# A three-stage fp32 network on one core: the gates of two token blocks from seven products of halves in place of eight

## The chip, the cores and the metric

One core of a Trainium2 chip runs the whole program in one launch. The metric is the device time of one execution in microseconds (us): the median of three runs is 1384.78 us.

## The reference

Retention attention (8 heads, 576 positions, 8 sequences) gives `x`; a mixer adds a low-rank mix of positions and a 512-2048-512 ReLU layer; a last stage makes the output. Its lines, on 4608 tokens (8 x 576) of 512 features:

```python
x_prev = np.concatenate([np.zeros((B, 1, D), dtype=np.float32), x[:, :-1, :]], axis=1)
xk = mu_k * x + (1.0 - mu_k) * x_prev
xr = mu_r * x + (1.0 - mu_r) * x_prev
k = np.maximum(xk @ w_k, 0.0)
v = k * k @ w_v
r = 1.0 / (1.0 + np.exp(-(xr @ w_r)))
return (r * v).astype(np.float32)
```

The change touches `r`: the product of `xr` with the 512 x 512 weight `w_r`, called the gates.

## The kernel before, in words

Features lie on the 128 partitions, tokens along the free axis, in 9 blocks of 512 tokens. Every fp32 product is made of three fp32r matmuls (128 x 512 out): the operands are split into a high half (a cast on ACT) and a low half (a subtraction on DVE or POOL), and weight high x token high, weight low x token high, weight high x token low are added in PSUM. Every instruction stands in its engine's queue in the order in which the Python code issues it (`manual_schedule`, L1002), so a waiting instruction holds back all that come after it on its engine.

Three stages follow one another. Up to about 565 us the attention, the low-rank mix and the first layer run; weights of later stages come in as 64-bit floats and are converted beside them, by jobs in the list `waiting`, of which `slot` (L135) runs one stage of each job that is under way. A job is load, `down` (ACT), `fill` (DVE), splits, and a store of the halves to DRAM ("parked"). `w_r` is parked by `Weight.park` (L172), `w_k` by `key_weight` (L208) with the four sums of its quarter blocks that products of halves need. `second_weight` (L348) brings in the weights of the second layer. Up to about 870 us the second layer runs over four pairs of blocks, seven products of half blocks for eight (`products`, L488); then the ninth block is done plainly (`project`, L583) to 914 us.

From 914 us on the last stage goes over the four pairs of blocks (L1316), then over the ninth block alone:
- `gate_tile` (L1186) makes the gates of one block and one quarter of the features: 12 matmuls into one PSUM bank, then a sigmoid on ACT. A pair has 8 of these, so 96 matmuls. Its weights `wru` stay in SBUF from 880 us to the end.
- `key_group` (L1207) makes one of four groups of 256 key features of both blocks, by seven products of halves of 6 matmuls each, and its results are squared and split (`square`, L1199). Its weights `wk` are fetched for each group.
- `value_part` (L1266) multiplies one group's squares with `w_v`, 24 matmuls into four banks `v`; after the fourth part of a block DVE multiplies `v` with the gates (L1284) and the result goes out.

The order for a pair is: 8 gate tiles, key groups 0 and 1, value part 0 of the even block, key group 2, value part 1, key group 3, value parts 2 and 3, then four value parts of the odd block. The gates use 8 banks: four that the pair's key groups will use (`mine`) and four (`other`).

The token operands of the next pair are made beside this by the generator `prepare` (L639), and `pump(n)` (L78) issues its next n steps. For each block and feature quarter a step scales the shifted tokens on ACT (`tp`, L623), another mixes them on DVE (L633) and casts the high half on ACT, a third subtracts the low half on DVE; then the operands of the keys follow, with sums and differences of half blocks (11, 22, 21, t1 to t4).

Of the kernel before, what the change touches and what calls it, by code (L numbers as in the profile page):

```python
# [39 lines left out]
def retention_mixer_kernel(ctx: ExitStack, tc: tile.TileContext, io):  # L40
# [158 lines left out]
    wr = Weight("wr", io["moe2_w_r"])  # L199
    later_weights = [wr, *wv]  # L200
# [5 lines left out]
    kept_k = [dram.tile([128, 2, 2, 4, 256], F32, name=f"keys{g}") for g in range(NG)]  # L206

    def key_weight(g, pool):  # L208
        raw, a, got = [], [], {}

        def load():
            for i in range(2):
                r = pool.tile([128, 512], I64, tag="unit", name=f"wkraw{g}_{i}")
                c0 = (g + NG * i) * 128
                nc.sync.dma_start(
                    r.rearrange("p (k n) -> p k n", n=128),
                    io["moe2_w_k"][:, c0:c0 + 128].rearrange("(k p) n -> p k n", p=128),
                )
                raw.append(r)
# [9 lines left out]
        def fill(i):  # L229
            if i == 0:  # L230
                got["f"] = unit(pool, F32, f"wkf{g}")
# [26 lines left out]
        def parts(i):  # L258
            h, l = (
                pool.tile([128, 4, 256], F32R, tag="unit", name=f"wk{x}{g}_{i}") for x in "hl"  # L260
# [11 lines left out]
        def store(i):  # L272
            for lo, x in enumerate(got[i]):
                for w in range(2):
                    nc.sync.dma_start(
                        kept_k[g][:, w, lo, 2 * i:2 * i + 2], x[:, 2 * w:2 * w + 2].bitcast(F32)
                    )
# [9 lines left out]
    def load_keys(n):  # L287
        for i, w in enumerate((wkp, wkq)):
            w[n] = []
            for lo in range(2):  # L290
                x = big.tile([128, 4, 256], F32R, tag="unit", name=f"wk{n}_{i}{lo}")
                nc.sync.dma_start(x.bitcast(F32), kept_k[n % NG][:, i, lo])
                w[n].append(x)

# [53 lines left out]
    def second_weight(j, pool):  # L348
# [66 lines left out]
        def parts_of_one(i):  # L415
# [4 lines left out]
            load, *[None] * (5 if late else 1), down, lambda: fill(0), lambda: fill(1), sums,  # L420
# [180 lines left out]
    def finish(t):  # L601
        u = uraw.pop(t)
        for o in range(KD):
# [33 lines left out]
    xr, xk = {}, {}  # L637

    def prepare(q):  # L639
        ts = blocks(q)  # L640
        for t in ts:
            h = [unit(big, F32R, f"rh{t}_{i}") for i in range(2)]
            l = [unit(big, F32R, f"rl{t}_{i}") for i in range(2)]
            xr[t] = h, l
            for k in range(KD):
                tp = shifted(t, 1, k)
                yield
                m = small(F32, f"m{t}_{k}")
                mixing(m, t, 1, k, tp)
                hk, lk = h[k // 2][:, k % 2, :], l[k // 2][:, k % 2, :]  # L650
                nc.scalar.copy(hk, m)
                yield
                nc.vector.tensor_tensor(lk, m, hk.bitcast(F32), op=ALU.subtract)
                yield

        def split(nm, src):
            h, l = unit(big, F32R, f"kh{nm}_{q}"), unit(big, F32R, f"kl{nm}_{q}")
            xk[q, nm] = h, l
            nc.scalar.copy(h, src)
            yield  # L660
            nc.vector.tensor_tensor(l, src, h.bitcast(F32), op=ALU.subtract)
            yield


        def half(t, i):
            for k in (2 * i, 2 * i + 1):
                tp = shifted(t, 0, k)
                yield
                mixing(x2b[t][i][:, k % 2, :], t, 0, k, tp)
                yield  # L670

        a = x2b[ts[0]]
        yield from half(ts[0], 0)
        yield from split("11", a[0])
        if len(ts) == 2:
            b = x2b[ts[1]]
            yield from half(ts[1], 0)
            yield from half(ts[1], 1)
            yield from split("22", b[1])
            t3 = unit(big, F32, f"t3_{q}")  # L680
            nc.vector.tensor_tensor(t3, b[1], b[0], op=ALU.subtract)
            yield
            yield from split("t3", t3)
            nc.vector.tensor_tensor(b[0], b[0], a[0], op=ALU.subtract)
            yield
            yield from split("t1", b[0])
            nc.vector.tensor_tensor(b[1], b[1], b[0], op=ALU.subtract)
            yield
            yield from split("t2", b[1])
        yield from half(ts[0], 1)  # L690
        yield from split("21", a[1])
        if len(ts) == 2:
            nc.vector.tensor_tensor(a[1], a[1], b[1], op=ALU.subtract)
            yield
            yield from split("t4", a[1])
# [7 lines left out]
    with ExitStack() as st:  # L703
# [482 lines left out]
    def gate_tile(t, o, base):  # L1186
        xh, xl = xr[t]
        ps = bank(base + o, f"r{t}_{o}")
        ops = [(lo, x, k) for k in range(KD) for lo, x in ((0, xh), (1, xh), (0, xl))]
        for j, (lo, x, k) in enumerate(ops):  # L1190
            nc.tensor.matmul(  # L1191
                ps, wr.part(lo, k, col(o)), x[k // 2][:, k % 2, :],
                start=(j == 0), stop=(j == len(ops) - 1),
            )
        if o % 2 == 0:
            gate[t, o // 2] = unit(big, F32, f"g{t}_{o}")
        nc.scalar.activation(gate[t, o // 2][:, o % 2, :], ps, AF.Sigmoid)
# [9 lines left out]
    def key_group(n, base):  # L1207
# [3 lines left out]
        wp_, wq_ = wkp.pop(n), wkq.pop(n)  # L1211
        plan = {
            1: ("a", wp_, 0, "11"), 7: ("c", wp_, 3, "t3"), 5: ("d", wp_, 2, "t1"),
            2: ("b", wp_, 1, "21"), 6: ("a", wq_, 2, "t2"), 4: ("c", wq_, 1, "t4"),
            3: ("d", wq_, 3, "22"),
        }
        kept = {}
        for m in (1, 7, 5, 2, 6, 4, 3):
            b, w, wi, nm = plan[m]
            xh, xl = xk[q, nm]  # L1220
            for i in range(2):
                wh, wl = (v[:, wi, col(i)] for v in w)
                for j, (l, r) in enumerate(((wh, xh), (wl, xh), (wh, xl))):
                    nc.tensor.matmul(  # L1224
                        ps[b], l, r[:, i, :], start=(m in (1, 7, 5, 2) and i == 0 and j == 0),
                        stop=(i == 1 and j == 2), skip_group_check=True,
                    )
# [38 lines left out]
    def value_part(t, g, base):  # L1266
        if g == 0:
            vacc[t] = [bank(base + o, f"v{t}_{o}") for o in range(KD)]
        do_late()
        kh, kl = kk.pop((t, g))  # L1270
# [18 lines left out]
    for p in range(NF // 2):  # L1289
# [12 lines left out]
        if p == 0:  # L1302
            for t in blocks(0):
                load_x2(t, big2)
            background.append(prepare(0))
# [10 lines left out]
    for q in range(NB // 2 + 1):  # L1316
# [3 lines left out]

        for x, t in enumerate(ts):
            for o in range(KD):
                gate_tile(t, o, (mine, other)[x])
                pump(3)
            del xr[t]
        pump(1000)
        if not last:
            PUMP[0] = 0
            for g in range(NG):
# [18 lines left out]
        else:  # L1348
            PUMP[0] = 0
# [75 lines left out]
```

## Time and profile before

| | |
|---|---|
| median of 3 runs | 1384.78 us |
| the three runs | 1384.33, 1384.78, 1390.41 us |
| the profiled execution: its own time | 1388.45 us |
| its span, first to last instruction | 1386.0 us |
| PE busy | 1357.9 us, 98% |
| PE weight loads busy | 1105.0 us, 80% |
| DVE busy | 853.4 us, 62% |
| ACT busy | 589.0 us, 42% |
| POOL busy | 342.4 us, 25% |

PE is TensorE's matmuls, DVE VectorE, ACT ScalarE, POOL GpSimd, SP the queue that issues the DMAs. A PE that is busy may still be held back by other things, since ends of matmuls are modelled, so the starts of the matmuls are what to read. Line numbers are those of the kernel before.

### The profile page before, as it was taken

How to read it: one execution, taken by the hardware profiler on the slowest of the kernel's cores; microseconds unless marked ns; L12 is line 12 of the kernel's file. 1: busy time of each engine (PE TensorE's matmuls, PEld its weight loads, DVE VectorE, ACT ScalarE, POOL GpSimd, SP SyncE). 2: the span in 40 equal slices, each digit the busy share in tenths (PEclk: the TensorE clock that was granted, in tenths of full speed). 3: DMA queues.
4: the chain of work that ended last, by engine and by line, in shares of the span. 5: the costliest groups of instructions: out<-in, count | busy, mean ns of one | idle time of the engine just before them, and what ended most of it. 6: DMA issues, size and time to landing. Idle time of an engine off the chain costs nothing.

```text
span 1386.0 us, 25620 instructions
## 1 busy us (share of the span) xinstructions
PE 1357.9 (98%) x10236; PEld 1105.0 (80%) x10236; DVE 853.4 (62%) x1249; ACT 589.0 (42%) x1021; POOL 342.4 (25%) x273
## 2 busy tenths in 40 slices
PE   6899999999999999999999999999999999999998
PEld 4677777777877878888888888888888888888887
DVE  6874445344422256999797988675666666666622
ACT  4443334343332354554454434553354454454421
POOL 3250231323210045222221222203303303304200
PEclk8799999999999999999999999999999999999999
DMA  9667586968753456969788886855234234233250
GB/s 342 229 224 240 180 294 230 303 235 290 258 182 119 146 191 233 330 212 298 258 296 289 273 295 219 308 203 197 89 113 164 92 114 160 91 117 126 92 213 31
DMA packets 114822, 286.61 MB, mean 207 GB/s; under 512 B 14352, under 2 KB 24976, under 8 KB 114704
## 3 DMA queue, kind: packets, MB, share of 16 engines
q1 hardware_dynamic: 114704, 284.99, 59.7%
q8 instruction: 80, 1.31, 0.4%
q14 instruction: 38, 0.31, 0.1%
HBM read 195.82 MB, written 89.13 MB: 206 GB/s over the span
## 4 chain that ended last, share of the span: by engine, by line
PE 62%; DVE 2%; DMA 1%; issue 0%; DVEq 0%
PE v L1275 14%; PE r L1191 7%; PE gc L510 6%; PE ga L510 6%; PE gd L510 6%; PE h L325 6%; PE kd L1224 3%; PE kc L1224 3%; PE ka L1224 3%; PE gb L510 3%; PE k L1258 2%; PE kb L1224 2%; PE c L592 1%; PE c L590 1%; PE c L591 1%; DMA t<-ra 1%
## 5 line engine op out<-in xcount | busy, mean ns | idle before, releaser
L331 ACT ACTIVATE hs<-h 128x512 f32<-128x512 f32 x144 | 85.7, 598 | 251.9 <-PE h L325 244.3
L775 DVE TENSOR_TENSOR pm<-up,dtab 128x256 f32<-128x256 f32 x72 | 30.4, 422 | 153.7 <-PE up L788 140.3
L1205 POOL TENSOR_TENSOR vl<-m,vh 128x512 fp32r<-128x512 f32 x32 | 41.4, 1295 | 264.3 <-ACT vh L1204 241.0
L469 ACT CAST sbh<-rb 128x1024 fp32r<-128x1024 f32 x64 | 67.4, 1053 | 51.7 <-PE gd L510 41.6
L1275 PE MATMUL v<-vh,wv_0u 128*128 128x512 f32 x288 | 88.7, 389 | 0.0
L1275 PE MATMUL v<-vh,wv_1u 128*128 128x512 f32 x288 | 88.7, 389 | 0.0
L1191 PE MATMUL r<-rh,wru 128*128 128x512 f32 x288 | 88.7, 389 | 0.0
L470 DVE TENSOR_TENSOR sbl<-rb,sbh 128x1024 fp32r<-128x1024 f32 x64 | 85.3, 1333 | 2.2 <-ACT sbh L469 2.1
L470 DVE TENSOR_TENSOR sal<-ra,sah 128x1024 fp32r<-128x1024 f32 (+1 forms) x64 | 65.4, 1022 | 16.8 <-PE gd L510 9.0
L469 ACT CAST sah<-ra 128x1024 fp32r<-128x1024 f32 (+1 forms) x64 | 53.5, 837 | 52.1 <-DVE ra L451 26.2
L1275 PEld LDWEIGHTS v<-vh,wv_1u 128*128 128x128 f32 x288 | 54.1, 188 | 11.2
L1191 PEld LDWEIGHTS r<-rh,wru 128*128 128x128 f32 x288 | 54.1, 188 | 11.2
L1275 PEld LDWEIGHTS v<-vh,wv_0u 128*128 128x128 f32 x288 | 54.1, 188 | 11.2
L1205 POOL TENSOR_TENSOR vl<-c,vh 128x512 fp32r<-128x512 f32 x32 | 55.2, 1746 | 22.5 <-ACT vh L1204 22.5
L918 DVE TENSOR_TENSOR xt<-mx,xt 128x256 f32<-128x256 f32 x64 | 28.8, 457 | 51.8 <-PE mx L914 51.8
L1191 PE MATMUL r<-rl,wru 128*128 128x512 f32 x144 | 56.0, 389 | 0.0
L1275 PE MATMUL v<-vl,wv_0u 128*128 128x512 f32 x144 | 56.0, 389 | 0.0
L1275 PE MATMUL v<-vl,wv_1u 128*128 128x512 f32 x144 | 56.0, 389 | 0.0
L734 POOL TENSOR_TENSOR kv<-kv,ktab 128x512 f32<-128x512 f32 (+1 forms) x40 | 41.4, 1036 | 53.6 <-DMA kv<-in_kv 47.0
L554 POOL TENSOR_TENSOR x<-x,ur 128x512 f32<-128x512 f32 x16 | 24.9, 1569 | 109.9 <-DMA ur<-ub 53.8
L623 ACT ACTIVATE tp<-x2l,omu 128x511 f32<-128x511 f32 x72 | 51.5, 717 | 0.8 <-DMA x2l<-xb 0.8
L1234 DVE TENSOR_TENSOR m<-kb,m 128x512 f32<-128x512 f32 x16 | 11.1, 691 | 62.3 <-PE kb L1224 60.3
(253 smaller groups left out, 3642.0 us busy)
## 6 DMA issues: line engine op xcount, KB each, us to landing
wk<-keys SPq DMA_DIRECT2D x80, 512.0 KB, 5.6
hp<-hs SPq DMA_DIRECT2D x128, 256.0 KB, 3.3
rb<-hp SPq DMA_DIRECT2D x64, 512.0 KB, 6.0
qk<-in_qk SPq DMA_DIRECT2D x32, 512.0 KB, 4.6
kv<-in_kv SPq DMA_DIRECT2D x32, 512.0 KB, 5.8
ra<-hp SPq DMA_DIRECT2D x32, 512.0 KB, 7.1
ur<-ub SPq DMA_DIRECT2D x18, 512.0 KB, 6.2
x2l<-xb SPq DMA_DIRECT2D x18, 512.0 KB, 7.6
```

What stands on the lines that cost most here:

```text
L325: nc.tensor.matmul(hps[t, f], w.part(lo, k, fo), u[k // 2][:, k % 2, :], start=(part == 0 and k == 0), stop=(part == 2 and k == KD - 1),)
L331: nc.scalar.activation(h, hps.pop((t, f)), AF.Relu)
L469: nc.scalar.copy(hi_, src)
L470: nc.vector.tensor_tensor(lo_, src, hi_.bitcast(F32), op=ALU.subtract)
L510: nc.tensor.matmul(group[g][p], l[:, col(p)], r, start=(h == 0 and j == 0 and i == 0), stop=(i == 2 and last), skip_group_check=True,)
L623: nc.scalar.activation(tp[:, 1:], x[:, :BT - 1], AF.Copy, scale=omu[:, j, k:k + 1])
L734: nc.gpsimd.tensor_tensor(k, k, ktab[:, p, :n].to_broadcast([128, n, NP, D]), op=ALU.mult)
L775: nc.vector.tensor_tensor(m, t[:, :, 0:128].rearrange("p g (a i) -> p g a i", i=L), dtab, op=ALU.mult)
L1191: nc.tensor.matmul(ps, wr.part(lo, k, col(o)), x[k // 2][:, k % 2, :], start=(j == 0), stop=(j == len(ops) - 1),)
L1205: eng.tensor_tensor(l, x, h.bitcast(F32), op=ALU.subtract)
L1224: nc.tensor.matmul(ps[b], l, r[:, i, :], start=(m in (1, 7, 5, 2) and i == 0 and j == 0), stop=(i == 1 and j == 2), skip_group_check=True,)
L1275: nc.tensor.matmul(vacc[t][o], w.part(lo, g, col(o)), x[:, i, :], start=(g == 0 and i == 0 and j == 0), stop=(g == NG - 1 and i == 1 and j ...
```

## The change

The gates of a pair are made like the keys. `prepare_mixed` mixes the tokens of both blocks into tiles `mr`, now beside value parts 0 and 1 of the pair before; `operands` makes the seven split operands from them, and later the same for the keys from `x2l`. `gates` runs seven products for two groups of 256 gate features: 84 matmuls for a pair in place of 96. Four of the products are copied from PSUM by ACT, ten additions on DVE join them, and the sigmoid then reads SBUF. The ninth block keeps its plain 48 matmuls. The gate weights are parked with their sums by two jobs of the kind that parks the keys' weights, behind those of `w_v`; seven empty jobs space the list. They are fetched anew for each pair (8 loads of 512 KB). The keys' first weights are fetched at the pair's start in place of the end of the pair before. The first job of the second layer's weights waits one slot longer, and the ninth block's evictions in `finish` change places.

```diff
     NG = DF2 // 256
     kept_k = [dram.tile([128, 2, 2, 4, 256], F32, name=f"keys{g}") for g in range(NG)]
-
-    def key_weight(g, pool):
+    kept_r = [dram.tile([128, 2, 2, 4, 256], F32, name=f"gates{g}") for g in range(2)]
+
+    def block_weight(g, pool, src, kept, kind):
...
+    def load_gates(q):
+        for i, w in enumerate((wrp, wrq)):
+            for g in range(2):
+                w[q, g] = []
+                for lo in range(2):
+                    x = big.tile([128, 4, 256], F32R, tag="unit", name=f"wr{q}_{g}_{i}{lo}")
+                    nc.sync.dma_start(x.bitcast(F32), kept_r[g][:, i, lo])
+                    w[q, g].append(x)
...
-            load, *[None] * (5 if late else 1), down, lambda: fill(0), lambda: fill(1), sums,
+            load, *[None] * (5 if late else 1 if j else 2), down, lambda: fill(0), lambda: fill(1), sums,
...
-        for o in range(KD):
+        for o in (2, 0, 1, 3):
             x2 = small(F32, f"x2_{t}_{o}")
...
+    def mixed(q, j, out):
+        ts = blocks(q)
+        for t, i in [(t, 0) for t in ts] + [(t, 1) for t in ts[::-1]]:
+            ks = (2 * i, 2 * i + 1)
+            tps = [shifted(t, j, k) for k in ks]
+            for k, tp in zip(ks, tps):
+                mixing(out[t][i][:, k % 2, :], t, j, k, tp)
+                yield
+
+    def operands(x, q, a, b, nm):
+        def upper(n, src):
+            h, l = unit(big, F32R, f"{nm}h{n}_{q}"), unit(big, F32R, f"{nm}l{n}_{q}")
+            x[q, n] = h, l
+            nc.scalar.copy(h, src)
+            return lambda: nc.vector.tensor_tensor(l, src, h.bitcast(F32), op=ALU.subtract)
...
+        t = unit(big, F32, f"{nm}t_{q}")
+        less(t, b[1], b[0])
+        yield
+        lower()
+        lower = upper("t3", t)
+        yield
+        less(b[0], b[0], a[0])
+        yield
+        lower()
+        lower = upper("t1", b[0])
+        yield
...
     def prepare(q):
...
+        a, b = (*blocks(q), None)[:2]
+        yield from operands(xr, q, mr.pop(a), b and mr.pop(b), "r")
+        yield from mixed(q, 0, x2b)
+        yield from operands(xk, q, x2b.pop(a), b and x2b.pop(b), "k")
...
-        for w in later_weights:
+        for w in wv:
             w.park(big)
-        for g in range(NG):
-            waiting.insert(4 * g, key_weight(g, big))
+        jobs = [block_weight(g, big, io["moe2_w_k"], kept_k, "k") for g in range(NG)]
+        jobs += [block_weight(g, big, io["moe2_w_r"], kept_r, "r") for g in range(2)]
+        for at in (9, 10, 11, 13, 15, 17, 19):
+            waiting.insert(at, [None])
+        for at, job in zip((0,4,8,12,16,20), jobs):
+            waiting.insert(at, job)
...
+    PLAN = {
+        1: ("a", 0, 0, "11"), 7: ("c", 0, 3, "t3"), 5: ("d", 0, 2, "t1"), 2: ("b", 0, 1, "21"),
+        6: ("a", 1, 2, "t2"), 4: ("c", 1, 1, "t4"), 3: ("d", 1, 3, "22"),
+    }
...
+    def gates(q, bases, steps):
...
+        for m in PLAN:
+            b = PLAN[m][0]
+            for g in range(2):
+                if b not in ps[g]:
+                    ps[g][b] = bank(bases[g] + "abcd".index(b), f"r{b}{q}_{g}")
+                x = product(m, w[g], xr, q, ps[g])
+                if m in (1, 7, 5, 6):
+                    kept[m, g] = small(F32, f"r{m}_{q}_{g}")
+                    nc.scalar.copy(kept[m, g], x)
...
+            del xr[q, PLAN[m][3]]
+            pump(steps)
...
-        if p in (1, 2):
-            wr.load(big2, p - 1)
-        if p == 4:
+        if p == 6:
+            load_gates(0)
+        if p == 7:
             load_keys(0)
-        pump(6 if p else 0)
+        pump(4 if p else 0)
...
+        if q:
+            load_keys(q * NG)
         if not last:
-            PUMP[0] = 0
+            gates(q, (mine, other), 1 if q else 2)
+            PUMP[0] = 2
...
                 key_group(n, mine)
-                if g > 0:
+                if g == 0:
+                    pump(1000)
+                    PUMP[0] = 0
+                    background.append(prepare_mixed(q + 1))
+                else:
                     if g == NG - 1:
...
-                        load_keys(n + 1)
                         background.append(prepare(q + 1))
-                        PUMP[0] = 3
-                    value_part(ts[0], g - 1, other)
+                        PUMP[0] = 2
+                    value_part(ts[0], g - 1, other, 3 if g < NG - 1 else 0)
             value_part(ts[0], NG - 1, other)
             for g in range(NG):
+                if g == 1:
+                    load_gates(q + 1)
                 value_part(ts[1], g, mine)
```

Three places show how the queues move. First DVE at the end of the first pair, up to the first eviction of the odd block's values (`o` from `v`), before; `m` is a mixed quarter, `rl` a low half of a gate operand, `tp` the shifted tokens, `x2l` the tokens, which the keys' mixing overwrites:

```order
L633 SCALAR_TENSOR_TENSOR m_3_10774<-x2l_1_10288,mu,tp_1_3_10770 128x512
L653 TENSOR_TENSOR rl_1_10709<-m_3_10774,rh_1_10707 128x512
L629 MEMSET tp_0_0_10790 128x1
L633 SCALAR_TENSOR_TENSOR x2l_0_10283<-x2l_0_10283,mu,tp_0_0_10790 128x512
...
L633 SCALAR_TENSOR_TENSOR x2l_0_10287<-x2l_0_10287,mu,tp_0_1_10833 128x512
L629 MEMSET tp_0_2_10850 128x1
L633 SCALAR_TENSOR_TENSOR x2l_1_10288<-x2l_1_10288,mu,tp_0_2_10850 128x512
L1284 TENSOR_TENSOR o_0_10855<-v_0_10690,g_0_10143 128x512
```

And the same place in the change, where `rt` and `kt` are differences of half blocks and `rlt` their low halves:

```order
L644 SCALAR_TENSOR_TENSOR mr_1_10439<-x2l_1_10346,mu,tp_1_3_10698 128x512
L668 TENSOR_TENSOR rt_10719<-mr_1_10441,mr_0_10440 128x1024
L665 TENSOR_TENSOR rl_1_10717<-mr_0_10438,rh_1_10716 128x1024
L668 TENSOR_TENSOR mr_0_10440<-mr_0_10440,mr_0_10438 128x1024
L665 TENSOR_TENSOR rlt_1_10723<-rt_10719,rht_1_10722 128x1024
...
L644 SCALAR_TENSOR_TENSOR x2l_1_10346<-x2l_1_10346,mu,tp_0_3_10911 128x512
L668 TENSOR_TENSOR kt_10932<-x2l_1_10350,x2l_0_10349 128x1024
L665 TENSOR_TENSOR kl_1_10930<-x2l_0_10345,kh_1_10929 128x1024
L668 TENSOR_TENSOR x2l_0_10349<-x2l_0_10349,x2l_0_10345 128x1024
L1354 TENSOR_TENSOR o_0_10951<-v_0_10774,g_0_10177 128x512
```

The sums of the gates and the first three operations of the keys' sums now stand ahead of the eviction, and each low half stands one operation behind the source of the next cast.

Second, ACT in the first stage, in the sequence whose attention is worked on at 330 us (`xs` copies a tile out of PSUM that PE needs back, `ca` is the `down` of a weight, `hs` the ReLU of the first layer), before:

```order
L227 ACTIVATE ca<-wkraw_1_4295 128x512
L331 ACTIVATE hs_5_4527<-h_5_4514 128x512
L127 CAST wv_1p_4288<-cf 128x512
L104 ACTIVATE ca<-wv_raw_4470 128x512
L873 COPY xs_3_4583<-xn_3_4578 128x512
L331 ACTIVATE hs_6_4598<-h_6_4585 128x512
```

And in the change:

```order
L227 ACTIVATE ca<-wkraw_1_4287 128x512
L342 ACTIVATE hs_5_4517<-h_5_4504 128x512
L895 COPY xs_3_4569<-xn_3_4564 128x512
L342 ACTIVATE hs_6_4584<-h_6_4571 128x512
L342 ACTIVATE hs_7_4600<-h_7_4587 128x512
```

The `down` of a tile of `w_v` is gone from in front of the copy.

Third, ACT where the first weights of the second layer (`w2a`) come in, before:

```order
L331 ACTIVATE hs_0_6338<-h_0_6325 128x512
L331 ACTIVATE hs_1_6354<-h_1_6341 128x512
L367 ACTIVATE w2a_6357<-w2raw_0_6321 128x512
L367 ACTIVATE w2a_6357<-w2raw_1_6323 128x512
L331 ACTIVATE hs_2_6373<-h_2_6360 128x512
```

And in the change:

```order
L342 ACTIVATE hs_0_6373<-h_0_6360 128x512
L342 ACTIVATE hs_1_6389<-h_1_6376 128x512
L342 ACTIVATE hs_2_6405<-h_2_6392 128x512
L378 ACTIVATE w2a_6408<-w2raw_0_6356 128x512
L378 ACTIVATE w2a_6408<-w2raw_1_6358 128x512
```

The two `w2a` stand one ReLU later.

## Rows read from the trace of the kernel before

**Rows 1.** The page's head and its first part: busy time, share, instructions.
```profile
span 1386.0 us, 25620 instructions
PE 1357.9 (98%) x10236; PEld 1105.0 (80%) x10236; DVE 853.4 (62%) x1249; ACT 589.0 (42%) x1021; POOL 342.4 (25%) x273
```
**Rows 2.** Chain of waits, last stage: start us, us, engine, tile, line, instructions.
```profile
985.06 32.64 PE v L1275 x144
1017.70 21.76 PE r L1191 x96
...
1371.30 8.85 PE v L1275 x39
1380.17 2.73 DVE o L1284 x4
```
**Rows 3.** Windows: PE, PEld, DVE, ACT, POOL busy, PE's granted clock, DMA share, GB/s.
```profile
1000.00:1050.00 50.00, 50.00 (x223) 41.40 (x222) 34.95 (x55) 26.86 (x50) 1.44 (x2) 1.00 0.47 169
```
**Rows 4.** Waits of PE, whole span: total us, times, longest.
```profile
PE xn L863 <- ACT xs L873: 6.0, 3, 3.0
PE h L325 <- ACT hs L331: 1.5, 1, 1.5
```
**Rows 5.** Groups of weight loads, 910 to 1386 us: busy us, mean ns.
```profile
L1191 PEld LDWEIGHTS r<-rh,wru 128*128 128x128 f32 x288 | 54.1, 188 | 11.2
```
**Rows 6.** Timeline of PE in the first stage: start, us; idle before and releaser.
```profile
331.35 0.63 PE L863 MATMUL xn<-ident,xt 128*64 128x128 f32 x4 [1.47 <-ACT xs L873]
...
487.50 1.20 PE L325 MATMUL h<-uh,w_0h 128*128 128x512 f32 x4 [1.52 <-ACT hs L331]
```
**Rows 7.** Timeline of ACT at the same two places.
```profile
330.17 0.66 ACT L104 ACTIVATE ca<-wv_raw 128x512 f32<-128x512 f32 x1 [7.29 <-DMA wv_raw<-in_moe_w_v]
...
483.80 0.66 ACT L367 ACTIVATE w2a<-w2raw 128x512 f32<-128x512 f32 x1 [2.54 <-DMA w2raw<-in_moe_w_ch]
486.30 0.66 ACT L367 ACTIVATE w2a<-w2raw 128x512 f32<-128x512 f32 x1 [1.84 <-DMA w2raw<-in_moe_w_ch]
486.86 1.08 ACT L331 ACTIVATE hs<-h 128x512 f32<-128x512 f32 x2
```
**Rows 8.** Timeline of DVE, first pair's end and second pair's start.
```profile
988.32 1.66 DVE L1203 SCALAR_TENSOR_TENSOR m<-m 128x512 f32<-128x512 f32 x1
...
991.60 0.95 DVE L633 SCALAR_TENSOR_TENSOR m<-x2l,mu,tp 128x512 f32<-128x512 f32 x1 [0.21 <-ACT tp L625]
...
1016.50 0.75 DVE L633 SCALAR_TENSOR_TENSOR x2l<-x2l,mu,tp 128x512 f32<-128x512 f32 x1
...
1017.37 0.75 DVE L633 SCALAR_TENSOR_TENSOR x2l<-x2l,mu,tp 128x512 f32<-128x512 f32 x1
...
1018.92 2.48 DVE L1284 TENSOR_TENSOR o<-v,g 128x512 f32<-128x512 f32 x4
...
1023.76 1.23 DVE L661 TENSOR_TENSOR kl<-x2l,kh 128x1024 fp32r<-128x1024 f32 x1 [1.12 <-ACT kh L659]
1024.90 1.22 DVE L681 TENSOR_TENSOR t<-x2l,x2l 128x1024 f32<-128x1024 f32 x1
...
1042.24 1.23 DVE L661 TENSOR_TENSOR klt<-x2l,kht 128x1024 fp32r<-128x1024 f32 x1 [1.12 <-ACT kht L659]
1045.00 0.69 DVE L1234 TENSOR_TENSOR m<-kb,m 128x512 f32<-128x512 f32 x1 [1.54 <-PE kb L1224]
```
**Rows 9.** Timeline of ACT at the same boundary.
```profile
1015.01 0.72 ACT L623 ACTIVATE tp<-x2l,omu 128x511 f32<-128x511 f32 x1
...
1015.82 0.71 ACT L623 ACTIVATE tp<-x2l,omu 128x511 f32<-128x511 f32 x1
```
**Rows 10.** DMA issues, 915 to 1330 us: KB each, median us to landing.
```profile
wk<-keys SPq DMA_DIRECT2D x67, 512.0 KB, 5.0
...
wv_1u<-wv_kept SPq DMA_DIRECT2D x4, 512.0 KB, 10.9
```
**Rows 11.** Timeline of SP's queue at the same boundary.
```profile
1001.49 20.27 SPq L1285 DMA_DIRECT2D out<-o  x8
```

More of the change, by code (lines that the diff above doesn't have):

```diff
@@ L259, in parts @@
             h, l = (
-                pool.tile([128, 4, 256], F32R, tag="unit", name=f"wk{x}{g}_{i}") for x in "hl"
+                pool.tile([128, 4, 256], F32R, tag="unit", name=f"w{kind}{x}{g}_{i}") for x in "hl"
             )
@@ L635, in mixing @@
         )
-    xr, xk = {}, {}
-    def prepare(q):
[L640 to L695, printed above, removed]
@@ new lines, in retention_mixer_kernel, with less @@
+    xr, xk, mr = {}, {}, {}
+    def mixed(q, j, out):
[12 more added lines that the diff above has]
+            return lambda: nc.vector.tensor_tensor(l, src, h.bitcast(F32), op=ALU.subtract)
+        def less(out, u, v):
+            nc.vector.tensor_tensor(out, u, v, op=ALU.subtract)
+        lower = upper("11", a[0])
+        if b is None:
+            other = upper("21", a[1])
+            lower()
+            yield
+            other()
+            yield
+            return
+        t = unit(big, F32, f"{nm}t_{q}")
[5 more added lines that the diff above has]
+        less(b[0], b[0], a[0])
+        yield
+        lower()
+        lower = upper("t1", b[0])
+        yield
+        less(t, b[1], b[0])
+        yield
+        lower()
+        lower = upper("21", a[1])
+        two = upper("t2", t)
+        yield
+        lower()
+        yield
+        less(a[1], a[1], t)
+        yield
+        two()
+        lower = upper("t4", a[1])
+        yield
+        two = upper("22", b[1])
+        lower()
+        yield
+        two()
+        yield
@@ L1184, in do_late, with product @@
             late.pop(0)()
-    def gate_tile(t, o, base):
-        xh, xl = xr[t]
+    PLAN = {
+        1: ("a", 0, 0, "11"), 7: ("c", 0, 3, "t3"), 5: ("d", 0, 2, "t1"), 2: ("b", 0, 1, "21"),
+        6: ("a", 1, 2, "t2"), 4: ("c", 1, 1, "t4"), 3: ("d", 1, 3, "22"),
+    }
+    def product(m, w, x, q, ps):
+        b, part, wi, nm = PLAN[m]
+        xh, xl = x[q, nm]
+        for i in range(2):
+            wh, wl = (v[:, wi, col(i)] for v in w[part])
+            for j, (l, r) in enumerate(((wh, xh), (wl, xh), (wh, xl))):
+                nc.tensor.matmul(
+                    ps[b], l, r[:, i, :], start=(part == 0 and i == 0 and j == 0),
+                    stop=(i == 1 and j == 2), skip_group_check=True,
+                )
+        return ps[b]
@@ L1210, in key_group @@
         ps = {nm: bank(base + i, f"k{nm}{n}") for i, nm in enumerate("abcd")}
[L1211 to L1216, printed above, removed]
-        kept = {}
[L1218 to L1227, printed above, removed]
+        w = wkp.pop(n), wkq.pop(n)
+        kept = {}
+        for m in PLAN:
+            b = PLAN[m][0]
+            product(m, w, xk, q, ps)
             if m in (1, 7, 5, 6):
@@ L1264, in key_tile, with value_part @@
         square(t, g, i, a, nc.vector)
-    def value_part(t, g, base):
+    def value_part(t, g, base, more=0):
         if g == 0:
@@ L1269, in value_part @@
         do_late()
+        pump(more)
         kh, kl = kk.pop((t, g))
```

63 lines of the change are left out of this document (43 added, 20 removed).

## The prediction

> **What bounds the kernel now.** I read the first part of the page, then the chain, the windows of the last stage, the waits of PE, and the timelines of DVE, ACT and SP where two pairs meet. PE is busy for 98% of the span [rows 1]. The chain shows what that means in the last stage: from 985.06 to the end it is PE without a gap, until four multiplications on DVE [rows 2]. There the matmuls set the pace: 96 gate matmuls take 21.76 us, 144 value matmuls 32.64 us, both 0.2267 us a matmul [rows 2]. Of 50 us, DVE works 34.95, ACT 26.86 and POOL 1.44, the DMA engines are at 0.47, and PE's clock is granted in full, the 2.4 GHz level [rows 3]. So a matmul less is 0.2267 us less, as long as what feeds PE keeps up. In the first stage PE does wait: 6.0 us in three waits for ACT's copy of the tile `xn`, and 1.5 us for a ReLU [rows 4]; the windows of all else read leave PE full.
>
> **The sum.** It is made against the profiled execution, 1388.45 us (span 1386.0 and 2.45 around it), which lies 3.67 us above the median of the three runs; I carry the differences over to the median.
>
> 1. *Matmuls removed.* Each of four pairs has 84 for 96: 48 x 0.2267 = **10.88 us** less, 2.72 a pair, all on the path [rows 2].
>
> 2. *A ReLU no longer held.* At 483.80 and 486.30 ACT waits 2.54 and 1.84 us for the raw second-layer weights to land; the ReLU behind them leaves at 486.86 and PE stands 1.52 us [rows 6, 7]. In the change the two `w2a` stand one ReLU later (2.72 us, a layer tile of 12 matmuls), when the first has landed; the second can hold ACT to 486.96, but the ReLU behind it frees a bank that PE wants only 2.7 us later. Less **1.52 us**.
>
> 3. *A copy no longer held.* At 330.17 ACT has waited 7.29 us for a tile of `w_v`; the copy of `xs` behind it comes late and PE stands 1.47 us [rows 6, 7]. In the change that `down` is not there. Less **1.47 us**. The other two of these waits keep their place with `w_v` for `w_r`, a tile of the same size, and I leave them.
>
> 4. *Conversion with sums.* `w_r` now goes through the jobs that the keys' weights have: the same casts on ACT and fills on DVE, eight sums and eight subtractions on POOL, sixteen stores. They fall between 330 and 470 us, where POOL is the least used engine [rows 1] and no job of this kind shows among PE's waits [rows 4]. Zero; bounds: nothing gained, and at most a wait like the two others, up to 3.0 us [rows 4].
>
> 5. *Weights fetched for each pair.* Eight loads of 512 KB come in SP's queue behind the even block's outputs, of which the last goes at about 1003, and ahead of the odd block's [rows 11]. SP needs some 0.4 us a load, so the four that the first products use are issued by 1004.8 and, with the longest landing seen here, 10.9 us [rows 10], are there at 1015.7; PE wants them at 1017.70 [rows 2]. The other four land by 1017.4, wanted 10.9 us later. The keys' first four go behind the odd block's outputs, at 1021.9 to 1023.5, and land by 1034.4 at the worst; they are wanted at 1036.74. Zero, with 2 us to spare in both places.
>
> 6. *What stands ahead of the eviction of the odd block's values.* This is the one place where I find a new wait. Before, the first gate tiles of a pair used four banks that had long been free. Now the seventh matmul needs the first bank of the odd block's `v`, which DVE has to empty, 6 x 0.2267 = 1.36 us after the gates begin: at 1017.70 + 1.36 = 1019.06. I walk DVE's new queue. It is free at 988.32 + 1.66 = 989.98; before, its first mixing starts at 991.60 behind one `tp` of ACT [rows 8]. Two mixings now want two `tp`, which follow each other by 1015.82 - 1015.01 = 0.81 [rows 9]: the second starts at 992.4 at the earliest, and both are done at about 993.7. Then eleven operations on 1024 columns at 1024.90 - 1023.76 = 1.14, with four evictions at 2.48 / 4 = 0.62 among them [rows 8]: 12.5 + 2.5, to 1008.7. No low half waits for its cast, since another operation of 1.14 stands between and the cast takes about as long. ACT can begin the eight `tp` of the keys 1.4 us sooner, at 1007.3: 8 x 0.81 = 6.5, to 1013.8; the last two mixings end 1.5 later, 1015.3. Three operations of the keys' sums, 3.4: 1018.7. The eviction, 0.7, ends at 1019.4. PE waits about 0.4 us in each of the three boundaries between pairs: plus **1.2 us**. Low end: if ACT never paced DVE, ten mixings at 1017.37 - 1016.50 = 0.87, fourteen operations at 1.14 and four at 0.62 make 27.1, so 1017.1, and no wait. High end: if each of the eight low halves waits 1.12 us for its cast, as before [rows 8], 9.0 more at each boundary, so 3 x 9.4 = 28.2 in all. I take the walk, because the order shows the operation in between that was missing before.
>
> 7. *Ten additions and the first key group.* The additions (0.69 each [rows 8], 6.9 a pair) wait for products two, four and three of the gates and stand in DVE's queue among the keys' sums. The last sum's low half comes out at about 1041.5 by the same walk; product three of the first key group wants it at 1036.74 + 0.4 + 8.16 = 1045.3. Before, DVE was done at 1042.24 + 1.23 = 1043.5, with less than 2 us idle after it [rows 8]. Zero, at 3 us to spare. The banks of products one and seven are copied by ACT long before PE adds to them again, 10.9 us on.
>
> 8. *First and ninth block.* At 914 us the ninth block's second eviction-bank, the one the gates want first, is now emptied first, 1.36 us before it is wanted; DVE has nothing else due then. The ninth block itself is as before. Zero.
>
> Sum: -10.88 - 1.52 - 1.47 + 1.2 = -12.7. The profiled execution would become 1375.8, and the median 1384.78 - 12.7 = **1372.1 us**.
>
> A rule against rows: a removed matmul is worth 0.2267 us here [rows 2]. The Trainium skill (TensorE: Matmul & The Clock Gate, Back-to-back issue gap) gives about 131 ns as the sustained spacing of pairs of weight load and 512-column matmul, and about 216 ns without the loads. By 131 ns the 48 would be worth 6.3 us and the estimate 1376.7. The trace disagrees, with 227 ns over stretches of 96 and 144, and I follow it.
>
> **The rivals.**
> - *The first stage gives nothing.* New casts of `w_r` in ACT's queue hold `xs` copies as those of `w_v` did, and points 2 and 3 come back as waits elsewhere: 1372.1 + 3.0 = 1375.1. For it: three waits of PE for a copy of `xs` are in the trace [rows 4], and one of them stands behind a `down` [rows 7]. Against: the new jobs leave a slot between load and `down`. 17%.
> - *DVE is later at the boundary than I walk.* If two of the eight low halves wait 1.12 us, 3 x 2.24 = 6.7 more: 1378.8. For it: DVE has only 0.4 us less than nothing to spare there. 13%.
> - *The first key group takes back what the gates gave.* The keys' sums end no sooner than before while PE comes 2.72 us earlier, and PE waits there in three pairs: 10.88 - 3 x 2.72 = 2.72 left of point 1, so 1384.78 - 2.72 - 2.99 + 1.2 = 1380.3. Against it: 3 us to spare in point 7. 7%.
> - *Slower.* DVE's queue serialises with ACT's at the boundary, all eight low halves wait: 1384.78 - 13.87 + 28.2 = 1399.1. It decides from 13.87 / 3 = 4.6 us a boundary, that is from four of the eight. For it: before, every low half waits [rows 8]. Against: the order. 5%.
> - *A matmul less is worth less.* If weight loads paced PE, a pair of load and matmul would be worth 0.188 us [rows 5], 48 x 0.188 = 9.0, so 1374.0. Against: the spacing of 0.2267 with PE full. 3%.
>
> **The numbers.** Forecast 55%, 1372.1, by itself between 1370 and 1374.5. A measurement of this kernel can tell about 0.5% from no change, 6.9 us: below 1377.9 is faster, above 1391.7 slower. Faster: 55 + 17 + 3, and 5 of the 13 where fewer low halves wait: 80%. Slower: 4 of the 5. Same: 16%. The range 1369.0 to 1379.5 takes in the first two rivals, the low end of point 6 and the small run-to-run spread; it leaves out the key group (7), slower (5), the upper part of late DVE (4) and a few per cent below.
>
> **What would show it.** Right: 84 gate matmuls in 19.04 us for each pair; two waits of PE for `xs` in place of three and none for a ReLU at 487; a wait of PE for an eviction of `v` of under 1 us, at most, where a pair's gates begin; the gates' weights landed before. Wrong: waits of PE on low halves of gates or keys, on `wr` loads, on copies `xs` between 380 and 460, or a gap ahead of the first key group.

## The result, and the profile after

The changed kernel takes 1373.03 us, the median of six runs (1372.28 to 1376.18), beside 1386.6 us for six runs of the kernel before (1384.33 to 1390.41). The ratio is 0.9906, with a 95% interval of 0.9893 to 0.9920; by this ratio the change saves 13.0 us, between 11.1 and 14.8. The forecast was 12.7 us less and 1372.1 us. So the total came out, but not by its own list. Two of its terms are right to a tenth of a microsecond, a third was not there, and 0.7 us came from outside the span, where the forecast expected nothing.

The profiled execution took 1373.66 us with a span of 1371.9; before it was 1386.0 [rows 1]. So 1.8 us of an execution lie outside the span, where it was 2.45. In the spans I compare stretch by stretch. The chain of waits of the change, columns start, length, engine, tile, line, instructions:

```profile
978.04 32.64 PE v L1345 x144
1010.68 1.36 PE ra L1223 x6
1012.04 0.02 issue
1012.06 1.67 PE ra L1223 x6
1013.74 2.74 PE rc L1223 x12
...
1079.04 32.64 PE v L1345 x144
```

A pair now takes 1079.04 - 978.04 = 101.00 us. Before it took 103.36 (two such rows lay 1088.42 - 985.06 apart). Seven products for eight should give 2.72 a pair and gave 2.36; the rest, 0.36, is nearly all in the second group of `ra`, six matmuls in 1.67 us where 1.36 is their pace. From the first gate matmul to the end of the span, the last stage took 1371.88 - 909.88 = 462.00 us, before 1386.01 - 914.17 = 471.84: **9.84 less**, where points 1 and 6 together said 9.68.

What PE waits for where a pair's gates begin, from the timeline of PE and then that of DVE at the first boundary (start, busy time, what, and in brackets the idle time before it):

```profile
1010.52 0.62 PE L1223 MATMUL ra<-rh,wr 128*128 128x512 f32 x2
...
1011.20 0.61 PE L1223 MATMUL ra<-rh,wr 128*128 128x512 f32 x2
1011.65 0.39 PE L1223 MATMUL ra<-rl,wr 128*128 128x512 f32 x1
1012.06 0.74 PE L1223 MATMUL ra<-rh,wr 128*128 128x512 f32 x2
```
```profile
985.16 1.42 DVE L644 SCALAR_TENSOR_TENSOR mr<-x2l,mu,tp 128x512 f32<-128x512 f32 x2
...
1007.92 1.22 DVE L668 TENSOR_TENSOR kt<-x2l,x2l 128x1024 f32<-128x1024 f32 x1
1009.06 1.21 DVE L665 TENSOR_TENSOR kl<-x2l,kh 128x1024 fp32r<-128x1024 f32 x1
1010.20 1.21 DVE L668 TENSOR_TENSOR x2l<-x2l,x2l 128x1024 f32<-128x1024 f32 x1
1011.33 2.48 DVE L1354 TENSOR_TENSOR o<-v,g 128x512 f32<-128x512 f32 x4
...
1033.33 1.23 DVE L665 TENSOR_TENSOR kl<-x2l,kh 128x1024 fp32r<-128x1024 f32 x1 [0.51 <-ACT kh L664]
```

The seventh matmul is due at 1010.52 + 6 x 0.2267 = 1011.88. DVE's first eviction ends at 1011.33 + 2.48 / 4 = 1011.95, and PE goes on at 1012.06; the matmuls behind it lose another 0.15. At this boundary no low half on DVE waits for its cast ahead of the eviction, as walked in point 6. The walk holds step by step: counted from the pair's first gate matmul (1017.53 before, 1010.52 now), each end that it names lies within 0.5 us of the trace. The last low half of the keys (`kl`) is done at 1034.56. Product three of the first key group, which wants it, starts 8.16 us after that group's first matmul, at about 1038.1: 3.5 us to spare, where point 7 had 3.

The gates' weights are issued well ahead. SP's queue:

```profile
996.52 4.88 SPq L303 DMA_DIRECT2D wr<-gates x8
1012.04 2.13 SPq L1355 DMA_DIRECT2D out<-o x4
```

Eight loads, 4.7 to 10.9 us each to land in the last stage. The fourth lands at 1006.5, 4.1 us before the gates begin (point 5 said 2).

In the first stage, the waits of PE [rows 4] are now (us in total, times, longest):

```profile
PE xn L885 <- ACT xs L895: 3.1, 2, 1.7
...
PE h L336 <- ACT hs L342: 0.9, 1, 0.9
```

Two waits for a copy `xs` are left of three; the one at 331 us is gone. But a wait for the ReLU `hs` is still there. ACT and then PE at that place [rows 6, 7]:

```profile
482.76 0.66 ACT L378 ACTIVATE w2a<-w2raw 128x512 f32<-128x512 f32 x1 [2.50 <-DMA w2raw<-in_moe_w_ch]
484.64 0.67 ACT L378 ACTIVATE w2a<-w2raw 128x512 f32<-128x512 f32 x1 [1.22 <-DMA w2raw<-in_moe_w_ch]
485.21 1.06 ACT L342 ACTIVATE hs<-h 128x512 f32<-128x512 f32 x2
```
```profile
485.84 1.19 PE L336 MATMUL h<-uh,w_0h 128*128 128x512 f32 x4 [0.86 <-ACT hs L342]
```

### The profile page after: what moved, and what is told of

It reads as the page before. It is cut to its first block, busy times and chain, and to the rows that moved or that the text cites. A ratio compares the mean times of both kernels' runs of the same rounds, so it can differ in the third digit from the quotient of the medians.

```text
span 1371.9 us, 25735 instructions
## 1 busy us (share of the span) xinstructions
PE 1346.2 (98%) x10188; PEld 1094.7 (80%) x10188; DVE 902.5 (66%) x1299; ACT 616.0 (45%) x1051; POOL 353.2 (26%) x285
## 3 DMA queue, kind: packets, MB, share of 16 engines
q8 instruction: 80, 1.31, 0.4%
## 4 chain that ended last, share of the span: by engine, by line
PE 59%; DVE 2%; DMA 2%; issue 1%; ACT 0%; SPq 0%; DVEq 0%
PE v L1345 14%; PE h L336 5%; PE ga L521 5%; PE gc L521 5%; PE gd L521 5%; PE kd L1223 3%; PE kc L1223 3%; PE ka L1223 3%; PE gb L521 3%; DMA rb<-hp 2%; PE ra L1223 2%; PE rc L1223 2%; PE rd L1223 2%; PE kb L1223 2%; PE k L1327 2%; PE c L602 1%
## 5 line engine op out<-in xcount | busy, mean ns | idle before, releaser
L785 PEld LDWEIGHTS up<-qk 64*64 64x64 f32 x1152 | 24.7, 139 | 32.5 <-issue 28.3
L1285 ACT CAST vh<-m 128x512 fp32r<-128x512 f32 x32 | 19.9, 622 | 66.5 <-DVE m L1284 66.5
L538 POOL TENSOR_TENSOR m<-m,ur 128x512 f32<-128x512 f32 x8 | 12.3, 1562 | 123.6 <-ACT m L535 123.6
L336 PE MATMUL h<-uh,w_0h 128*128 128x512 f32 x144 | 42.0, 414 | 1.5 <-ACT hs L342 0.9
```

The costliest lines, as they stand in the source:

```text
L336: nc.tensor.matmul(hps[t, f], w.part(lo, k, fo), u[k // 2][:, k % 2, :], start=(part == 0 and k == 0), stop=(part == 2 and k == KD - 1),)
```

## The experiments

**Theory.** The last stage is paced by PE at 0.2267 us a matmul; the only thing given back there is the wait for DVE's eviction. **Rivals.** The matmuls are worth less (weight loads pace PE); the gain comes from the other parts of the change; the operands of the keys are nearly as late as PE. In the first stage: a wait follows a `down` that stands ahead of it in ACT's queue, or it follows the landing of the transfer, wherever that stands.

I give for each run the length of its last stage (from its first gate matmul to the end of the span), since this isolates it from the first stage, which differs by several us between executions of one order of instructions.

### Eight products again

```diff
                 x = product(m, w[g], xr, q, ps[g])
+                if m == 5:
+                    product(m, w[g], xr, q, ps[g])
```

> The changed kernel with product 5 of the gates made twice (the second overwrites the first): 96 gate matmuls for a pair again, all else as in the change. If a matmul on the path is worth its 0.2267 us, 48 more cost 10.88 us: 1373.0 + 10.9 = 1383.9 us. Rival, weight loads set the pace (0.188 us): +9.0, 1382.0. Rival, the gain came from somewhere else than the matmuls (operands made sooner, fewer waits): about 1373.

1384.33 us, ratio to before 0.9990 (0.9978 to 1.0001). Last stage 472.90, that is **10.90 longer** than the change's 462.00, for 48 x 0.2267 = 10.88. In the chain, product 5 now has 24 matmuls over the two groups in place of 12:

```profile
1017.59 2.74 PE rc L1223 x12
1020.33 5.44 PE rd L1223 x24
```

The gain is the matmuls', at their full spacing. With weight loads as the pace it would have been 9.0.

### Only the matmuls taken out of the kernel before

```diff
+    was = []
...
+        if t % 2 and o == KD - 1:
+            ops = []
+            ps = was[-1]
+        was.append(ps)
```

> The kernel before with the twelve matmuls of one gate tile in eight left out (the last quarter of the odd block's gates reads the bank of the quarter before it, so the output is not the reference's): 84 gate matmuls for a pair and no other part of the change. If the matmuls alone make the last stage's gain, 1386.6 - 10.9 = 1375.7 us, no wait of PE in the last stage, and the waits of the first stage as before (xs at about 208, 270 and 331 us, a ReLU at 487). Rival, the gain needs the other parts: less than 10.9.

1378.24 us, ratio 0.9942 (0.9926 to 0.9958). The last stage is 465.08: 6.76 shorter than before, not 10.88. The rival holds here. PE, ACT and DVE in the first key group of the second pair:

```profile
1036.83 0.73 PE L1230 MATMUL ka<-kht,wk 128*128 128x512 f32 x2 [1.06 <-ACT m L1236]
```
```profile
1034.75 1.05 ACT L659 CAST kht<-x2l 128x1024 fp32r<-128x1024 f32 x1 [2.06 <-DVE x2l L693]
1035.71 0.59 ACT L1203 ACTIVATE g<-r 128x512 f32<-128x512 f32 x1
1036.20 0.58 ACT L1236 COPY m<-ka 128x512 f32<-128x512 f32 x1
```
```profile
1035.84 1.23 DVE L661 TENSOR_TENSOR klt<-x2l,kht 128x1024 fp32r<-128x1024 f32 x1 [1.12 <-ACT kht L659]
```

ACT casts, DVE subtracts, DVE makes the next source, ACT casts again, each waiting for the other. That chain ends at 1037.1, which is 25.9 us after the pair's first gate matmul (1011.13). Before it was the same 25.9 (1043.47 [rows 8] less 1017.53), though PE now comes to the keys 2.72 us sooner. In front of the copy `m` that PE needs, the chain holds ACT. PE stands 1.06 us in each of three pairs and loses 1.37 (4.12 in all). So the 12 matmuls a pair alone are not worth their 2.72. In the change the last low half is done 24.0 us after the pair's first gate matmul (1034.56 - 1010.52), 1.9 us sooner. That this comes from its order of the preparation, with an operation between a cast and its subtraction, is argued from the timelines; no run has that order without the other parts of the change.

### Six and five products

Product 6, and then also product 4, is left out (the bank as it stands is copied or added):

```diff
-                x = product(m, w[g], xr, q, ps[g])
+                x = product(m, w[g], xr, q, ps[g]) if m not in (6, 4) else ps[g][b]
```

> The changed kernel without product 6 of the gates (72 matmuls for a pair; the odd block's gates and part of the even block's are not the reference's), all operands, copies and additions still made. If PE alone sets the pace and the first key group has over 2.72 us to spare, another 10.88 us go: 1362.1 us, and no wait of PE for a low half in a first key group. Rival, the operands of the keys are about as late as PE: waits there, up to 2.72 us in each of three pairs, 1362.1 + 8.2 = 1370.3.

> The changed kernel without products 6 and 4 of the gates (60 matmuls for a pair, gates not the reference's). PE comes to the first key group 5.44 us sooner than in the change, where the last low half of the keys has about 3.5 us to spare by the trace. If DVE's additions also come sooner with the products, the low half ends about 1032.9 where PE wants it at 1032.6: 1373.0 - 21.8 + 3 x 0.5 = 1352.8. If the low half ends no sooner than in the change: 1.9 us of wait in three pairs, 1357.0. Rival, no such limit: 1351.3.

Six: 1365.69 us, ratio 0.9857 (0.9836 to 0.9877), last stage 453.29, 8.71 shorter than the change; the 2.17 us that are missing from 10.88 are lost in the first pair. Five: 1366.23 us, ratio 0.9857 (0.9834 to 0.9880), last stage 453.27: **the second product left out gives nothing of its 10.88 us**. With six, PE waits only in the first pair, 1.63 us. With five, in every pair; here the second (PE):

```profile
1025.42 0.74 PE L1223 MATMUL kc<-kht,wk 128*128 128x512 f32 x2 [0.30 <-DVE g L1243]
...
1027.75 0.73 PE L1223 MATMUL kd<-kht,wk 128*128 128x512 f32 x2 [0.66 <-DVE g L1243]
...
1031.64 0.73 PE L1223 MATMUL ka<-kht,wk 128*128 128x512 f32 x2 [0.86 <-ACT m L1299]
```

So behind the change there is room for one product a pair (2.72 us: with six products no pair from the second on has a new wait) and for no more: the 3 to 3.5 us of point 7 were right in size. I had missed by what they end. It is not the last low half: the first waits of the key group are for banks, which DVE empties with the gates' additions (`g`) among the keys' sums, and for ACT's copies behind them. The expected 1352.8 to 1357.0 was too low by 9 us at the least.

### The eviction two operations later, and out of the way

```diff
         if g == NG - 1:
+            if t in (1, 3, 5):
+                pump(2)
             for o in range(KD):
```

> The changed kernel with two more steps of the next pair's preparation (two operations of 1.14 us on 1024 columns) issued on DVE ahead of the eviction of the odd block's values, in three pairs; nothing else changes. If that eviction is what PE waits for where a pair's gates begin (0.33 us in the trace), the wait grows by about 2.3 us each time: 1373.0 + 6.9 = 1379.9, with waits of PE for o of about 2.6 us. Rival, the 0.33 us is a wait for something else (a weight load, a DMA) and DVE has room there: 1373.

1383.96 us, ratio 0.9982 (0.9971 to 0.9994). The wait grew as expected, by 2.40, 2.35 and 2.52 us at the three boundaries: the eviction is what PE waits for. But the last stage is 10.76 longer, 3.5 more than these three. PE's timeline, then windows with PE, PEld, DVE, ACT, POOL busy, PE's granted clock, DMA share and GB/s:

```profile
1116.82 0.73 PE L1223 MATMUL ra<-rh,wr 128*128 128x512 f32 x2 [2.41 <-DVE o L1356]
1117.39 0.54 PE L1223 MATMUL ra<-rl,wr 128*128 128x512 f32 x1
1117.73 1.05 PE L1223 MATMUL ra<-rh,wr 128*128 128x512 f32 x2
```
```profile
1013.47:1016.00 2.53, 2.53 (x11) 2.11 (x12) 2.53 (x4) 0.79 (x2) 0.00 (x0) 1.00 0.69 257
...
1118.00:1121.00 3.00, 3.00 (x8) 2.31 (x8) 1.82 (x3) 1.70 (x3) 0.00 (x0) 0.52 1.05 342
1223.50:1227.00 3.50, 3.50 (x11) 2.69 (x10) 2.96 (x4) 3.06 (x4) 0.00 (x0) 0.54 1.02 283
```

After the second and the third stall the granted clock is at its lower level, 1.2 GHz, for some 3 us, and the matmuls follow each other at 0.43 us. That cost 1.5 and 1.7 us more; the last 0.3 lie behind the last matmul (from its start to the end of the span 4.59 us, in the change 4.26). After the first stall, as long, it stayed at 2.4 GHz.

The other way round, the first group makes two products before the second group begins, so that the bank is wanted 2.72 us after the start and not 1.36:

```diff
-        for m in PLAN:
+        for m, g in [(1, 0), (7, 0), (1, 1), (7, 1)] + [(m, g) for m in (5, 2, 6, 4, 3) for g in range(2)]:
             b = PLAN[m][0]
-            for g in range(2):
+            if True:
...
-            del xr[q, PLAN[m][3]]
-            pump(steps)
+            if g:
+                del xr[q, PLAN[m][3]]
+                pump(steps)
```

> The changed kernel with the gates' first group making two products (1 and 7) before the second group begins, so that the odd block's bank is wanted 2.72 us after the start in place of 1.36. If the wait for the eviction is all that is lost at a boundary, 3 x 0.33 = 1.0 us less: 1372.0, and no wait of PE for o. Rival, the wait moves to the next bank or to an operand not yet ready (t3): 1373.

1372.2 us, ratio 0.9901 (0.9884 to 0.9919). The last stage is 460.96, **1.04 shorter** than the change's, and PE does not stop at the boundary:

```profile
1011.49 0.39 PE L1223 MATMUL ra<-rl,wr 128*128 128x512 f32 x1
1011.71 0.62 PE L1223 MATMUL rc<-rht,wr 128*128 128x512 f32 x2
```

One us cannot be told from none by times of these runs; it is the trace that shows it, and it came out the same in the two later runs with this edit (460.95 and 460.96).

### The loads of the gate weights later

```diff
-                if g == 1:
+                if g == 3:
                     load_gates(q + 1)
```

> The changed kernel with the eight loads of a pair's gate weights issued two value parts (10.88 us) later. By the trace the first four land 4.1 us before PE wants the first; 10.88 later the fourth lands at about 1017.3 where PE wants it at 1012: a wait of about 5 us in three pairs, in which the wait for the eviction is hidden: 1373.0 + 3 x 4.7 = 1387. Rival, the loads are hidden anyway (they land faster when nothing else moves): 1373 to 1378.

1373.24 us, ratio 0.9904 (0.9885 to 0.9923): no difference, and no wait for `wr`. It doesn't speak for the rival, for nothing was moved. SP's queue in this run, whose pair begins at 1014.52:

```profile
1000.53 4.53 SPq L303 DMA_DIRECT2D wr<-gates x8
1016.05 2.13 SPq L1355 DMA_DIRECT2D out<-o x4
```

The loads go 14.0 us before the pair, just as in the change (1010.52 - 996.52). SP has no instruction between the two sets of outputs, so it takes the loads as soon as it is through with the first set, wherever the code issues them. How late they could come was not tried; the 4.1 us to spare stand as read from the trace.

### The first job of the second layer's weights

```diff
-            load, *[None] * (5 if late else 1 if j else 2), down, lambda: fill(0), lambda: fill(1), sums,
+            load, *[None] * (5 if late else 1), down, lambda: fill(0), lambda: fill(1), sums,
```

> The changed kernel with the first job of the second layer's weights undone to its place before (one slot sooner). The wait of PE for the ReLU hs was 1.52 us at 487.50 before and is 0.86 at 485.84 in the change. If the place of the two w2a in ACT's queue makes it, it is back at about 1.5, one layer tile sooner. Rival, it follows the landing of the raw weights and not the place: 0.9 or nothing.

A single run took 1376.91 us. The wait is **2.97 us**, twice what it was before, and the clock is at the lower level behind it (PE, then windows):

```profile
484.82 2.07 PE L336 MATMUL h<-uh,w_0h 128*128 128x512 f32 x4 [2.97 <-ACT hs L342]
```
```profile
486.00:488.00 2.00, 2.00 (x7) 1.52 (x6) 0.57 (x1) 0.00 (x0) 1.21 (x2) 0.50 0.91 283
```

Both expectations missed: neither 1.5 nor 0.9. So within the change the slot is worth over 2 us in this one trace, yet beside the kernel before it gains nothing. Something else in the change makes the raw tiles late. SP's queue in the change:

```profile
471.02 1.70 SPq L275 DMA_DIRECT2D gates<-wrh x2
472.82 2.40 SPq L275 DMA_DIRECT2D gates<-wrl x2
...
478.41 0.92 SPq L369 DMA_DIRECT2D w2raw<-in_moe_w_ch x2
```

The last four stores of the gate weights take SP from 471.02 to 475.22, ahead of the raw tiles. In the last run they are put behind the first two of those tiles (together with the two products first):

```diff
-            lambda: store(0), lambda: parts(1), lambda: store(1),
+            lambda: store(0), lambda: parts(1),
+            (lambda: held.append(lambda: store(1))) if kind == "r" and g else lambda: store(1),
...
         ticks.append(0)
+        if len(ticks) == 3:
+            held.pop()()
...
```

> The changed kernel with two products of the first group first (as in the run before that had it) and with the last four stores of the gate weights moved in SP's queue from ahead of the first two raw tiles of the second layer to behind them. If those stores, 4.3 us of SP's queue, are why a wait of PE for the ReLU hs stays in the change (0.6 to 1.1 us in its traces), the raw tiles land some 3 to 4 us sooner and the wait is gone: with the 1.0 us of the boundaries 1373.6 - 0.9 - 1.0 = 1371.7. Rival, the tiles land late because the DMA engines are busy: the wait stays, 1372.6.

1372.35 us (1369.63 to 1375.01), ratio 0.9905 (0.9887 to 0.9923). The wait is gone; ACT:

```profile
478.58 0.66 ACT L380 ACTIVATE w2a<-w2raw 128x512 f32<-128x512 f32 x1
480.11 0.67 ACT L380 ACTIVATE w2a<-w2raw 128x512 f32<-128x512 f32 x1 [0.87 <-DMA w2raw<-in_moe_w_ch]
480.78 0.60 ACT L344 ACTIVATE hs<-h 128x512 f32<-128x512 f32 x1
```

The first tile lands at 477.30, before ACT comes to it. The rival, busy DMA engines, is out: that tile still takes 4.9 us to land (4.3 in the change), it only leaves sooner. The wait of the change was made by its own stores in SP's queue.

### An empty slot in the jobs of w_v, three edits together, and the change again

```diff
-                waiting.append(convert(fetch, parts, 128, 512, store))
+                job = convert(fetch, parts, 128, 512, store)
+                job.insert(1, None)
+                waiting.append(job)
```

> The changed kernel with an empty slot between load and down in the eight jobs of w_v, as the jobs with sums have it. If the two waits of PE for the copy xs (1.36 and 1.74 us, at 205.76 and 267.70) come from a down that waits for its tile to land ahead of the copy, both go: 1373.0 - 3.1 = 1369.9. Rival, the tile or the buffers come later too and the wait moves: 1373.

1374.3 us, ratio 0.9914 (0.9895 to 0.9932). Both waits for `xs` are gone, and the time is not less. Matmul by matmul against the change, PE gains 1.31 and 1.76 us at the two places and loses 0.42, 0.37, 0.30, 1.29, 0.30 and 0.40 at others between 157 and 309 us. The largest, PE and then POOL:

```profile
246.31 0.46 PE L828 MATMUL dn<-kv 64*64 64x64 f32 x16 [1.03 <-POOL kv L758]
```
```profile
243.34 1.48 POOL L128 TENSOR_TENSOR wv_0p<-cf,wv_0p 128x512 fp32r<-128x512 f32 x1
244.76 1.49 POOL L758 TENSOR_TENSOR kv<-kv,ktab 128x512 f32<-128x512 f32 x1
```

The split of the tile moved along with its `down` and now stands in POOL's queue ahead of the scaling of `kv`. The rival was right: the wait moved to another engine.

> The changed kernel with the three edits together: the empty slot in the jobs of w_v, two products of the first group first, and the first job of the second layer's weights one more slot later. If the three waits are independent: -3.1, -1.0 and -0.9, 1368.0 us. Rival, waits move instead of going: 1370 to 1373.

1371.83 us (1371.25 to 1372.83), ratio 0.9897 (0.9878 to 0.9915). The 1368.0 of three independent waits was not reached; it is the rival's 1370 to 1373. Of its three edits the one at the boundary shows, last stage 460.95; the wait for the ReLU is gone too, and the empty slot gives and takes as above.

> The changed kernel again, beside the two versions made from it: 1373, with two waits of PE for xs, one for a ReLU and three for an eviction of o. What differs from the first trace of it is how far landings alone move the waits of the first stage.

1374.12 us (1372.71 to 1376.04), ratio 0.9911 (0.9892 to 0.9931), last stage 461.97. Its waits for `xs` are 1.10 and 1.57 us, for the ReLU 0.99. This and the two runs above shared a chip. The intervals of the ratios overlap, though only one of the five times with three edits is above the lowest of these six, so that the version with three edits is the faster one is likely by its trace and not shown by its times.

## Why the prediction was right, point by point

1. *Matmuls removed, 10.88.* Shown: put back they cost 10.90. The pace of 0.2267 us was the right price, and the 131 ns of the Trainium skill (TensorE: Matmul & The Clock Gate, Back-to-back issue gap), by which they would be worth 6.3, does not hold for this stream.
2. *A ReLU no longer held, 1.52.* **Wrong; this is the step that failed.** The prediction put the two `w2a` one ReLU later and took the landing of the raw tiles from the trace of before. But point 4 put its stores between 330 and 470 us, and the last four go at 471.02 to 475.22, in SP's queue ahead of these loads. The loads go 4.5 us later by PE's own progress: 3.7 us ahead of the matmul that waited at 487.50, in place of 8.2 (485.98 without the wait, less 477.74). The wait that stays is 0.58 to 1.08 us in eight traces with this order. In a second trace of the order before (the run with 84 matmuls) PE loses only 0.25 us there. So nothing can be said to have been gained.
3. *A copy no longer held, 1.47.* Right. The wait at 331 us is in both traces of the order before (1.47 and 1.46) and in none of those with the order of the change.
4. *Conversion with sums, zero.* ACT, DVE and POOL did hide it; SP's queue did not, as told under 2. I counted the stores and left out what they stand in front of.
5. *Weights fetched for each pair, zero.* Right, with 4.1 us to spare where 2 were worked out.
6. *The eviction, +1.2.* Right: 3 x 0.36 read from the pair's period, and 1.04 when it is taken away. The wait worked out by the walk of DVE's queue came within 0.1 us a boundary.
7. *Ten additions and the first key group, zero.* Right, and the room of 3 us too; its end is set by banks and copies, not by the low half.
8. *First and ninth block, zero.* Nothing there shows among the waits.

In the two profiles the sum was saved by the first stage. It ends 4.30 us sooner there (first gate matmul at 909.88 for 914.17) where points 2 and 3 said 2.99. Of that, 1.46 is point 3. The wait at 207.92 us, 3.04 before, is 0.58 to 1.78 in the traces of the change; but it is 1.50 in the second trace of the order before, too, whose first stage and second together end at 910.49. So most of the 4.30 is what one profile differs from the next, and the profile that I worked from had a long first stage: its span is 1386.0, while 48 runs of the kernel before on four chips have median spans of 1382.8 to 1383.7. The forecast also carried the 2.45 us outside the span over without a reason. They are 2.37 to 3.29 in all those 48 runs and 1.74 to 1.83 in the twelve of the change; what makes the difference of 0.7 stays open. Fewer matmuls alone do not, since the kernel before with 84 has 2.40 to 2.48. What the runs show as the change's own is 9.84 in the last stage, 1.46 in the first and 0.7 outside the span, 12.0 us: inside the interval of 11.1 to 14.8, and near the 11.6 between the medians when the change was run again (1385.72 - 1374.12). That the total met the forecast to a microsecond is luck in this part: 1.52 us that were not gained are made up by the 0.7 that the forecast did not have and by the spread of the runs.

Of the rivals, "the first key group takes back what the gates gave" is what the matmuls alone would have met (4.12 of 10.88), and in the change it does not appear. "DVE is later at the boundary" was made on purpose and cost more than priced.

## What to carry to other kernels

Ask of every added instruction what stands behind it in its queue, the DMA queue too: four stores that cost no engine anything made the next loads late. Work taken from the engine that sets the pace pays only while what feeds it has room, and that room is measured by leaving out one piece more, and then two. A wait found in one trace should be looked for in a second one before its removal is counted on.

## What the runs showed of the hardware that I had not expected

A stall of TensorE of 2.4 us can cost 1.5 to 1.7 us on top: the granted clock went to the 1.2 GHz level after it for some 3 us. A shorter one did so too: behind the 1.78 us at 208.71, in the run with the loads issued elsewhere, 0.51 was granted from 209.0 to 212.5. It is not certain to: of the three like stalls of one execution two did so and one didn't, the stall of 2.97 us at 484.82 did, and the one of 3.04 us at 207.92 before was followed by a clock of 1.00.

The granted clock of the first 60 us differs from one execution to the next (the change with its loads issued elsewhere in the code, then the last run; columns as above):

```profile
0.00:60.00 60.00, 44.38 (x875) 32.27 (x879) 36.73 (x87) 26.48 (x64) 15.75 (x20) 0.72 0.76 272
```
```profile
0.00:60.00 60.00, 43.23 (x927) 31.31 (x928) 40.25 (x93) 27.72 (x66) 18.49 (x22) 0.86 0.81 291
```

The first of these begins its gates at 913.88 us, the last run at 906.89. Matmul for matmul, 3.6 of these 7.0 us are there by 60 us; 2.3 come with the longer stall at 208.71 and the low clock behind it, 0.3 with the second wait for `xs`, and 1.0 with the ReLU that the last run does not wait for. The 3.6 are more than twice what the change is shown to have done to the first stage, and it is why last stages are compared here by their own length. The clock is not all of it: in eight executions with 0.80 granted over these 60 us, the 901st matmul starts between 56.44 and 59.18 us.
